# Block-sparse attention with a feed-forward layer on one core: V gathers moved between queues, first save on another queue, second batch's loads dealt out differently

## The chip, the core and the metric

The kernel runs on one core of a Trainium2 chip. A core has a matrix engine (PE), a vector engine (DVE), a scalar engine (ACT), a general engine (POOL, GpSimd), and SP, which here only issues transfers. Each works through its own instructions in order; they meet at semaphores. Transfers (DMAs) are issued by SP, ACT or POOL and carried by 16 DMA engines that all queues share. The metric is the device time in microseconds (us), here the median of three runs.

## The reference

Four batches, eight heads, 768 positions, 64 channels per head. Attention is computed under a block mask (blocks of 32 positions, 24 blocks): a block sees itself and its neighbours, the first and last block see and are seen by everything, and each block also sees three sampled blocks. The heads are put side by side, and a feed-forward layer follows on the 3072 x 512 result.

```python
mask = np.abs(blk_i - blk_j) <= 1
mask = mask | (blk_i == 0) | (blk_j == 0) | (blk_i == n_blocks - 1) | (blk_j == n_blocks - 1)
for qb in range(n_blocks):
    for kb in sampled_blocks[qb]:
        mask[qb*32:(qb+1)*32, kb*32:(kb+1)*32] = True
attn = softmax(np.where(mask, scale * (q @ k.T), -1e9))
x = heads_side_by_side(attn @ v)            # 3072 x 512
h = x @ w_in                                # 3072 x 1024
solu = h * softmax(h)
ln = (solu - mean(solu)) / sqrt(var(solu) + 1e-6) * g_ln
out = ln @ w_out                            # 3072 x 512
```

## The kernel before

**Tiling.** Heads are worked on in pairs, so there are 16 pairs, four to a batch. The program is one list of steps `s`, written out by hand: the loop from L785 goes through them, and whatever a step calls is put on each engine's queue in that order. Six steps make a pair (`SLOT`): in the steps of pair T the static scores are computed (`score_static`, L414: own blocks and first and last block), and in the next six its sampled scores (`score_rand`, L458), the products with V (`out_list` and `out_mms`, L475 and L506) and the division by the sum (`normalise`, L512). From step 33 (`MOE0`) the feed-forward layer's own 120 steps (`moe_step`, L622) are threaded between the attention's, one or two per step.

**Preparing a batch.** V is loaded in six parts of 256 KB (`load_v`), cast to bf16 (`cast_v`), and saved as a whole to a scratch in DRAM, `v_scr` (`save_v`, 780 KB). From there the sampled rows are fetched by block index: 22 query blocks, `inner` (11, three blocks each) and `edge` (11, three sampled and one neighbour), are gathered into the tile `vg` (`gather_v`, L385). A gather is done either on POOL by one indirect DMA with a column of row numbers (L403), or on SP by a load of the indices into registers and three (inner) or four (edge) copies of 32 rows (L396, L400); the argument `on` picks the engine. K and Q are loaded in eight parts of 384 KB (`load_kq`), cast (`cast_kq`), transposed on PE and copied out of the accumulator (`turn_kq`, L317); the sampled K blocks are then copied by index from the transposed K (`gather_k`, L366), most of it on DVE and ACT. `glob_k` and `glob_v` put aside the first and last block.

**What sets the order.** Each queue is in order: an instruction that waits holds all behind it on the same engine. Staging buffers couple the queues. The pool `raw` has four buffers for what is loaded, so the fifth load waits for the cast of the first; `stage` has two for what is cast, so the third cast waits for the first transpose. Each transfer on SP or ACT also takes one of eight semaphores, and waits until the transfer that had it before has landed. The two buffers of `vg` hold batch 0's raw V and raw K and Q first. The feed-forward weights `w_out` are loaded into `w_f`, which lies in the second buffers of the sampled K tiles, so batch 1's `gather_k` waits until they have been scaled (`scale_w`, L655).

**Batch 0** is loaded before the loop: V on SP (L693), then five parts of K and Q (L694 to L696), then four writes of a zero row block to the ends of the scratches (L713), three parts of Q on ACT (L768). V is cast on POOL and ACT in turn and saved on SP (L766). Its gathers stand in steps 2 and 3, odd ones on SP, even ones on POOL. **Batch 1** is prepared from step 4 on (L840 to L866, with `f` the step counted from the batch's start, three steps later for batch 1), on POOL's and SP's queues; batches 2 and 3 the same way 24 and 48 steps later. The weights are loaded at step 7 (`w_out`, `g_ln`, on SP) and step 15 (`w_in`, on POOL).

Of the kernel before, what the change touches and what calls it, by code (L numbers as in the profile page):

```python
# [201 lines left out]
def kernel(  # L202
# [11 lines left out]
    nc = tc.nc  # L214

    B, H, S, D = q.shape
# [85 lines left out]
    def load_kq(b, which, a, eng, rw=None):  # L302

        if rw is None:
            rw = raw.tile([TQ, 2, NT, D], FP32, tag="raw", name=f"raw{which}{b}_{a}")
        eng.dma_start(
            out=rw.rearrange("p h i d -> p h (i d)"),
            in_=(k, q)[which][b, 2 * a : 2 * a + 2].rearrange("h (p i) d -> p h (i d)", i=NT))
        staged[which, b, a] = rw

    def cast_kq(b, which, a, copy):
        rw = staged[which, b, a]
        st = stage.tile([TQ, NT, 2, D], BF16, tag="st", name=f"st{which}{b}_{a}")
        copy(out=st.rearrange("p i h d -> p h i d"), in_=rw)  # L314
        staged[which, b, a] = st
# [17 lines left out]
    def cast_v(b, c, copy):  # L333
        copy(out=vbuf[b % 2][:, c, :, 0:D],  # L334
             in_=staged.pop((2, b, c)).rearrange("p (h d) -> p h d", h=H))

    def save_v(b, lo, hi, eng):
        eng.dma_start(out=v_scr[b][lo * TQ : hi * TQ, :].rearrange("(c p) e -> p c e", p=TQ),
                      in_=vbuf[b % 2][:, lo:hi].rearrange("p c h e -> p c (h e)"))
# [315 lines left out]
    def scale_w(c):  # L655
        nc.vector.tensor_scalar(out=w_out_sb[:, c, :], in0=w_f[c // (KF // 2)][:, c % (KF // 2), :],
                                scalar1=g_ln_sb[:, c : c + 1], scalar2=None, op0=ALU.mult)
# [13 lines left out]
    def centre_w(c):  # L671
        nc.vector.tensor_sub(out=w_out_sb[:, c, :], in0=w_out_sb[:, c, :], in1=mean_sb[0])
# [18 lines left out]
    raw_kq = vgp.tile([TQ, 2 * NPR - 1, 2, NT, D], FP32, tag="vg", name="raw_kq")  # L691
    for c in range(NCH):
        load_v(0, c, nc.sync, raw_v[:, c, :])  # L693
    load_kq(0, 0, 0, nc.sync)  # L694
    for n, (which, a) in enumerate(((1, 0), (0, 1), (0, 2), (0, 3))):
        load_kq(0, which, a, nc.sync, raw_kq[:, n])  # L696
    for vb in vbuf:
        nc.vector.memset(vb[:, :, :, D:D1], 1.0)
    zero_v = prd_p.tile([TQ, 2 * n_ed * BLK], BF16, tag="prd1", name="zero_v")
    nc.vector.memset(zero_v, 0.0)  # L700


    band = setup.tile([TQ, NCH, TQ], BF16, name="band")
# [5 lines left out]
    for z in kgz:  # L709
        nc.vector.memset(z, 0.0)  # L710
    nc.vector.memset(soluT[:, :, :, 128:D2], 1.0)
    for b in range(B):
        nc.sync.dma_start(out=v_scr[b][NB * BLK :, :], in_=zero_v[0:BLK, 0 : H * D1])  # L713


    tab_k = setup.tile([TQ, NB, 4], I32, name="tab_k")
# [46 lines left out]
                                scalar1=sgn * BLK, scalar2=None, op0=ALU.add)  # L763
    for c in range(NCH):
        cast_v(0, c, (nc.gpsimd.tensor_copy, nc.scalar.copy)[c % 2])
    save_v(0, 0, NCH, nc.sync)  # L766
    for a in range(1, NPR):
        load_kq(0, 1, a, nc.scalar, raw_kq[:, 3 + a])  # L768
    for which, a in ((0, 0), (1, 0)):
# [15 lines left out]
    while step < N_STEPS:  # L785
        s += 1
        T, j = s // SLOT, s % SLOT
        pending = len(masks)

        if j < 2 and 1 <= T <= n_pairs:  # L790
            score_rand(T - 1, j)
        if 2 <= j < 5 and T < n_pairs:
            score_static(T, j - 2)

        if 1 <= T <= n_pairs and 1 <= j < 5:
            par = (j - 1) // 2
            if j % 2 == 1:
                lst = out_list(T - 1, par)
                out_mms(lst, 0, 3 * NCH + 1)
            else:  # L800
                out_mms(lst, 3 * NCH + 1, len(lst))
                normalise(T - 1, par)
                if par == 1 and (T - 1) % NPR == NPR - 1:
                    put_rows((T - 1) // NPR)
                    moe_x((T - 1) // NPR * 2)

        mask_all(pending)

        if s >= MOE0:
            for _ in range(2 if (s - MOE0) % 4 == 3 or T > n_pairs else 1):  # L810
                moe_step(step)
                step += 1

        for n in {0: (1, 2), 1: (3, 4), 3: (5,), 4: (6,)}.get(s, ()):
            which, a = ((0, 1), (0, 2), (0, 3), (1, 1), (1, 2), (1, 3))[n - 1]
            cast_kq(0, which, a, nc.vector.tensor_copy)
            turn_kq(0, which, a, (nc.scalar.copy, nc.vector.tensor_copy)[which])
        if s == 1:
            glob_k(0, nc.vector.tensor_copy)
            glob_v(0, nc.vector.tensor_copy)  # L820
        if s in (2, 3):
            for i in range((s - 2) * n_in, n_in + (s - 2) * n_ed):
                gather_v(0, i, on=i % 2)
        if 2 <= s < 6:
            for i in range((s - 2) * 6, min((s - 1) * 6, n_gk)):
                gather_k(0, i, on=(1, 2)[i % 2])

        if s == 15:
            nc.gpsimd.dma_start(out=w_in_sb, in_=moe_w_in.rearrange("(c p) f -> p c f", p=128))
        if s == 7:  # L830
            nc.sync.dma_start(out=g_ln_sb, in_=moe_g_ln.rearrange("(c p) -> p c", p=128))
            load_w()
        if 11 <= s < 11 + KF:
            scale_w(s - 11)
        if s == 24:
            mean_of_w()
        if 25 <= s < 25 + KF:
            centre_w(s - 25)

        for nb in range(1, B):  # L840
            f = s - (nb - 1) * 24
            if f == 4:
                alloc_kq(nb)
            f -= 3 if nb == 1 else 0
            for i in range(6):
                if f == 1 + i // 2:
                    load_v(nb, i, nc.sync)
                if f == 5 + i // 2:
                    cast_v(nb, i, nc.gpsimd.tensor_copy)
            for i in range(8):  # L850
                if f == 4 + i:
                    load_kq(nb, i // 4, i % 4, nc.sync)
                if f == 8 + i:
                    cast_kq(nb, i // 4, i % 4, nc.gpsimd.tensor_copy)
                if f == 11 + i:
                    turn_kq(nb, i // 4, i % 4, (nc.scalar.copy, nc.vector.tensor_copy)[i // 4])
            if f == 9:
                save_v(nb, 0, NCH, nc.sync)
                glob_v(nb, nc.gpsimd.tensor_copy)
            if f == 15:  # L860
                glob_k(nb, nc.gpsimd.tensor_copy)
            for i in range(n_gk):
                if f == 15 + i // 2:
                    gather_k(nb, i, on=(1, 2, 1, 2, 1, 0)[i % 6])
                if f == 12 + i * 13 // 22:
                    gather_v(nb, i, on=(0, 1, 0, 1, 0)[i % 5])  # L866
        if T == n_pairs + 1 and j == 0:
            nc.vector.tensor_scalar(out=okr[:, 0:n_r], in0=recip_all, scalar1=1e-25,
                                    scalar2=None, op0=ALU.is_ge)
            nc.vector.scalar_tensor_tensor(out=okr[:, 0:n_r], in0=recip_all, scalar=1e25,  # L870
                                           in1=okr[:, 0:n_r], op0=ALU.is_le, op1=ALU.mult)
            nc.vector.reduce_sum(out=n_ok[:, 0:1], in_=okr[:, 0:n_r], axis=AX.X)
# [48 lines left out]
```

## Time and profile before

| | |
|---|---|
| median of three runs | 331.94 us (330.65 to 333.08) |
| profiled execution | 334.93 us, of which 333.3 span |
| busy: PE, DVE, ACT, POOL | 231.7, 151.4, 159.1, 98.2 us |
| chain that ended last: PE, DMA, ACT, "issue", DVE | 44, 8, 8, 8 and 6% |
| first feed-forward product on PE (L555) | 121.3 us |
| gathers of V on POOL (L403) | 50, 971 ns each |
| copies of V rows on SP (L396) | 131 |

Times in the profile are us from the span's start, of one profiled execution. A stage is read from what each engine did in it and from what ended its waits; a wait is put down to what ended it last. "issue" is time in which an engine waited for nothing that the profile shows. In the table of stages the columns are length, busy time of PE, PEld (weight load), DVE, ACT and POOL with the number of instructions, granted PE clock, the share of the DMA engines' time and GB/s. In lists by time the columns are start, length, engine, line, instruction, count, and in brackets the idle time before and what ended it; SPq is SP's issuing of transfers.

### The profile page before, as it was taken

To read this page: it belongs to the slowest core of one execution; us is meant where nothing else is said; L and a number is where in the kernel's file an instruction comes from. 1 tells how busy PE (TensorE), PEld (TensorE's weight loads), DVE (VectorE), ACT (ScalarE), POOL (GpSimd) and SP (SyncE) were. 2 spreads that over 40 slices of the span, in tenths; PEclk is the share of its full clock that TensorE was granted. 3 is DMA by queue.
4 is the path that set the end of the run, shared out by engine and by line. 5 is a ranking of instruction groups with operands and counts; after the bars stand their busy time and mean duration, and the time that the engine had idled before them with its cause. 6 is when DMAs were issued, how large, how long until landed. Compare 5 with 4: busy or idle time off the path is not lost.

```text
span 333.3 us, 9097 instructions
## 1 busy us (share of the span) xinstructions
PE 231.7 (70%) x3452; PEld 149.2 (45%) x3466; DVE 151.4 (45%) x488; ACT 159.1 (48%) x328; POOL 98.2 (29%) x151
## 2 busy tenths in 40 slices
PE   0244122808693699946889998567999999889990
PEld 0233121506451456633466566334665755635450
DVE  7667101144460933643475346344644544536250
ACT  2378020408253546622594675236846746233530
POOL 2107500416867442786004337850000000000000
PEclk9999999999556559975899999759999999999998
DMA  7964324999937887455345985442031021043202
GB/s 144 321 227 104 98 53 93 186 384 278 235 86 172 177 244 254 116 107 160 110 99 112 308 273 111 131 130 71 5 80 65 10 74 65 2 112 75 100 30 71
DMA packets 65008, 45.62 MB, mean 137 GB/s; under 512 B 43040, under 2 KB 58752, under 8 KB 64960
## 3 DMA queue, kind: packets, MB, share of 16 engines
q1 hardware_dynamic: 57760, 30.72, 35.6%
q0 software_dynamic: 2928, 6.81, 8.3%
q10 hardware_dynamic: 4272, 7.47, 6.2%
q8 instruction: 28, 0.46, 0.6%
q14 instruction: 20, 0.16, 0.2%
HBM read 33.26 MB, written 9.62 MB: 129 GB/s over the span
## 4 chain that ended last, share of the span: by engine, by line
PE 44%; DMA 8%; ACT 8%; issue 8%; DVE 6%; SPq 4%; another core or an unknown queue 2%; POOL 2%; ACTq 1%; DVEq 0%; POOLq 0%
PE ops L608 11%; PE op L509 10%; PE hps L555 8%; PE sums L573 3%; ACT eT L562 3%; PE ps L468 3%; DMA raw<-in_k_dram 3%; DMA rawv<-in_v_dram 3%; PE tp L321 3%; SPq L396 2%; DMA v_scr<-v 2%; PE ps L437 2%; DVE soluT L563 2%; ACT ot L616 2%
## 5 line engine op out<-in xcount | busy, mean ns | idle before, releaser
L441 ACT ACTIVATE pst<-ps 128x1024 bf16<-128x1024 f32 x48 | 49.1, 1024 | 45.6 <-PE ps L437 36.2
L563 DVE TENSOR_TENSOR soluT<-hps,eT 128x384 bf16<-128x384 f32 x56 | 31.0, 558 | 60.2 <-ACT eT L562 58.7
L403 POOL DMA_INDIRECT vg<-v_scr,idx x50 | 48.5, 971 | 29.4 <-DVE kgi L379 13.8
L321 PE MATMUL tp<-ident,st 128*128 128x128 bf16 x192 | 20.4, 261 | 44.8 <-DVE st L314 14.8
L608 PE MATMUL ops<-w_out_sb,soluT 128*128 128x512 bf16 x179 | 47.2, 408 | 2.4 <-issue 2.0
L555 PE MATMUL hps<-xT,w_in_sb 128*128 128x384 bf16 x224 | 46.4, 334 | 3.4 <-ACT ot L616 2.3
L472 ACT ACTIVATE prd<-ps 96x768 bf16<-96x768 f32 (+1 forms) x32 | 24.0, 755 | 48.7 <-PE ps L468 20.3
L509 PEld LDWEIGHTS <-pst 64*128 64x128 bf16 (+3 forms) x608 | 31.3, 110 | 20.0 <-issue 7.2
L562 ACT ACTIVATE eT<-hps 128x384 bf16<-128x384 f32 x56 | 27.1, 490 | 23.3 <-PE hps L555 22.4
L321 PEld LDWEIGHTS <-st 128*128 128x128 bf16 x192 | 15.1, 116 | 50.0 <-issue 18.0
L520 DVE RECIPROCAL recip_all<-op 128x7 f32<-128x7 f32 x32 | 6.5, 203 | 61.5 <-PE op L509 52.9
L314 POOL CAST st<-raw 128x768 bf16<-128x768 f32 x24 | 20.2, 840 | 33.6 <-DMA raw<-in_k_dram 18.1
L509 PE MATMUL op<-vg,prd 96*32 96x65 bf16 (+1 forms) x704 | 18.8, 211 | 15.1 <-DMA vg<-v_scr 12.1
L509 PE MATMUL op<-v,pst 128*64 128x65 bf16 (+1 forms) x384 | 25.6, 211 | 5.0 <-issue 4.9
L555 PEld LDWEIGHTS <-w_in_sb 128*128 128x128 bf16 x256 | 21.3, 98 | 15.1 <-issue 4.4
L608 PEld LDWEIGHTS <-soluT 128*128 128x128 bf16 x192 | 18.1, 102 | 20.6 <-issue 4.8
L334 POOL CAST v<-rawv 128x512 bf16<-128x512 f32 x18 | 11.4, 654 | 49.5 <-DMA rawv<-in_v_dram 28.1
L324 DVE COPY qT<-tp 128x768 bf16<-128x768 bf16 x15 | 14.3, 953 | 19.4 <-PE tp L321 7.5
L509 PE MATMUL op<-vgl,pst 64*128 64x65 bf16 (+1 forms) x224 | 17.8, 209 | 7.2 <-DVE xb L521 6.2
L509 PEld LDWEIGHTS <-prd 96*32 96x32 bf16 (+1 forms) x704 | 12.6, 104 | 19.9 <-issue 9.9
L324 ACT COPY kT<-tp 128x768 bf16<-128x768 bf16 x16 | 12.7, 803 | 16.7 <-PE tp L321 16.7
L521 DVE TENSOR_TENSOR xb<-op,recip_all 128x448 bf16<-128x448 f32 x32 | 20.0, 624 | 1.2
(106 smaller groups left out, 313.3 us busy)
## 6 DMA issues: line engine op xcount, KB each, us to landing
out_dram<-ot ACTq DMA_DIRECT2D x24, 256.0 KB
raw<-in_k_dram SPq DMA_DIRECT2D x13, 384.0 KB
rawv<-in_v_dram SPq DMA_DIRECT2D x18, 256.0 KB
raw<-in_q_dram SPq DMA_DIRECT2D x12, 384.0 KB
vg<-v_scr SPq DMA_DIRECT2D x131, 32.5 KB
v_scr<-v SPq DMA_DIRECT2D x4, 780.0 KB
w_f<-in_moe_w_out_dram SPq DMA_DIRECT2D x2, 1024.0 KB
raw_v<-in_v_dram SPq DMA_DIRECT2D x6, 256.0 KB
```

The lines of the kernel that those rows point to most:

```text
L314: copy(out=st.rearrange("p i h d -> p h i d"), in_=rw)
L321: nc.tensor.matmul(tp[:, i, :], st[:, i, :], ident, is_transpose=True, start=(i == 0), stop=(i == NT - 1))
L324: copy(out=dst, in_=tp.rearrange("c i p -> c p i"))
L403: nc.gpsimd.indirect_dma_start(out=vgs[b][0:m, i, :], out_offset=None, in_=v_scr[b], in_offset=bass.IndirectOffsetOnAxis(ap=idx[0:m, qb : ...
L441: nc.scalar.activation(out=psts[pair][:, u], in_=ps, func=ACT.Exp, scale=scale)
L472: nc.scalar.activation(out=prds[pair, u], in_=ps[0:m, :, 0 : len(qbs) * BLK], func=ACT.Exp, scale=scale)
L509: nc.tensor.matmul(o, w, m, start=(i == 0), stop=(i == len(lst) - 1), skip_group_check=True)
L521: nc.vector.tensor_tensor(out=xbs[b][:, :, h * D : (h + 1) * D], in0=op[:, :, 0:D], in1=recip.broadcast_to([TQ, NSL, D]), op=ALU.mult)
L555: nc.tensor.matmul(hps, w_in_sb[:, c, f * 128 : (f + 1) * 128], xTs[g][:, c, :], start=(c == 0), stop=(c == KD - 1))
L562: nc.scalar.activation(out=eTs[g, f], in_=hps, func=ACT.Exp, scale=1.0)
L563: nc.vector.tensor_tensor(out=soluT[:, f, :, 0:128], in0=hps.rearrange("p (i x) -> p i x", i=GT), in1=eTs[g, f].rearrange("p (i x) -> p i ...
L608: nc.tensor.matmul(o_ps[t], soluT[:, f, i, 0:128], w_out_sb[:, f, :], start=(f == 0), stop=(f == KF - 1))
```

## The change

- Batch 0's save of V is issued on ACT's queue, behind ACT's casts. The four writes of zero rows come ahead of the K and Q loads on SP.
- Batch 0's gathers of V stand in steps 2 to 5 with its gathers of K, two of three on POOL: 15 on POOL and 7 on SP (11 and 11 before).
- Batch 1: V is loaded in steps 2 to 4, two parts a step, so between SP's gathers, and cast on DVE. K and Q are loaded in steps 5 to 9; K is cast on POOL, Q on DVE, and both are copied out of the accumulator on ACT. The save is at step 7.
- Batch 1's gathers of V run over steps 10 to 26, those of K over steps 21 to 29.
- In batches 1 to 3, too, 15 gathers of V are on POOL and 7 on SP (13 and 9 before).
- In batches 2 and 3 the loads, casts, transposes and gathers of K and Q come a step later, the gathers of V a step earlier.
- `w_out` and `g_ln` are loaded at step 10, behind batch 1's loads, `w_in` at step 12; scaling starts at step 17, the mean is at step 26, and centring takes four steps instead of eight.

```diff
     for c in range(NCH):
         load_v(0, c, nc.sync, raw_v[:, c, :])
-    load_kq(0, 0, 0, nc.sync)
-    for n, (which, a) in enumerate(((1, 0), (0, 1), (0, 2), (0, 3))):
-        load_kq(0, which, a, nc.sync, raw_kq[:, n])
...
     nc.vector.memset(zero_v, 0.0)
+    for b in range(B):
+        nc.sync.dma_start(out=v_scr[b][NB * BLK :, :], in_=zero_v[0:BLK, 0 : H * D1])
+    load_kq(0, 0, 0, nc.sync)
+    for n, (which, a) in enumerate(((1, 0), (0, 1), (0, 2), (0, 3))):
+        load_kq(0, which, a, nc.sync, raw_kq[:, n])
...
-    for b in range(B):
-        nc.sync.dma_start(out=v_scr[b][NB * BLK :, :], in_=zero_v[0:BLK, 0 : H * D1])
...
-    save_v(0, 0, NCH, nc.sync)
+    save_v(0, 0, NCH, nc.scalar)
...
-        if s in (2, 3):
-            for i in range((s - 2) * n_in, n_in + (s - 2) * n_ed):
-                gather_v(0, i, on=i % 2)
         if 2 <= s < 6:
             for i in range((s - 2) * 6, min((s - 1) * 6, n_gk)):
                 gather_k(0, i, on=(1, 2)[i % 2])
-
-        if s == 15:
-            nc.gpsimd.dma_start(out=w_in_sb, in_=moe_w_in.rearrange("(c p) f -> p c f", p=128))
-        if s == 7:
+                gather_v(0, i, on=(0, 1, 0)[i % 3])
+
+        if s == 10:
             nc.sync.dma_start(out=g_ln_sb, in_=moe_g_ln.rearrange("(c p) -> p c", p=128))
             load_w()
-        if 11 <= s < 11 + KF:
-            scale_w(s - 11)
-        if s == 24:
+        if s == 12:
+            nc.gpsimd.dma_start(out=w_in_sb, in_=moe_w_in.rearrange("(c p) f -> p c f", p=128))
+        if 17 <= s < 17 + KF:
+            scale_w(s - 17)
+        if s == 26:
             mean_of_w()
-        if 25 <= s < 25 + KF:
-            centre_w(s - 25)
+        if 27 <= s < 27 + KF // 2:
+            centre_w(2 * (s - 27))
+            centre_w(2 * (s - 27) + 1)
 
         for nb in range(1, B):
             f = s - (nb - 1) * 24
             if f == 4:
                 alloc_kq(nb)
-            f -= 3 if nb == 1 else 0
-            for i in range(6):
-                if f == 1 + i // 2:
+            first = nb == 1
+
+            lv, cv, lk, ck, tk = (2, 4, 5, 8, 9) if first else (1, 5, 4, 8, 11)
+            per = 2 if first else 1
+            pool_copy, dve_copy = nc.gpsimd.tensor_copy, nc.vector.tensor_copy
+            for i in range(NCH):
+                if f == lv + i // 2:
                     load_v(nb, i, nc.sync)
-                if f == 5 + i // 2:
-                    cast_v(nb, i, nc.gpsimd.tensor_copy)
-            for i in range(8):
-                if f == 4 + i:
-                    load_kq(nb, i // 4, i % 4, nc.sync)
-                if f == 8 + i:
-                    cast_kq(nb, i // 4, i % 4, nc.gpsimd.tensor_copy)
-                if f == 11 + i:
-                    turn_kq(nb, i // 4, i % 4, (nc.scalar.copy, nc.vector.tensor_copy)[i // 4])
-            if f == 9:
+                if f == cv + i // 2:
+                    cast_v(nb, i, dve_copy if first else pool_copy)
+            for i in range(2 * NPR):
+                if f == lk + (i + 1) // per:
+                    load_kq(nb, i // NPR, i % NPR, nc.sync)
+                if f == ck + (i + 1) // per:
+                    cast_kq(nb, i // NPR, i % NPR, dve_copy if first and i >= NPR else pool_copy)
+                if f == tk + (i + 1) // per:
+                    turn_kq(nb, i // NPR, i % NPR,
+                            nc.scalar.copy if first or i < NPR else dve_copy)
+            if f == 9 - 2 * first:
                 save_v(nb, 0, NCH, nc.sync)
-                glob_v(nb, nc.gpsimd.tensor_copy)
-            if f == 15:
-                glob_k(nb, nc.gpsimd.tensor_copy)
+                glob_v(nb, pool_copy)
+            if f == 16:
+                glob_k(nb, pool_copy)
             for i in range(n_gk):
-                if f == 15 + i // 2:
+                if f == (21 + i * 9 // n_gk if first else 16 + i // 2):
                     gather_k(nb, i, on=(1, 2, 1, 2, 1, 0)[i % 6])
-                if f == 12 + i * 13 // 22:
-                    gather_v(nb, i, on=(0, 1, 0, 1, 0)[i % 5])
+                if f == (10 + i * 17 // n_gk if first else 11 + i * 13 // n_gk):
+                    gather_v(nb, i, on=(0, 1, 0)[i % 3])
```

## The prediction

> **What bounds the kernel now.** I read the share of busy time by stage first, then PE's waits in the first 94 us, then SP's and POOL's instructions in order of time. Busy time by stage (length, then PE, PEld, DVE, ACT, POOL with counts, granted clock, DMA share, GB/s):
>
> ```profile
> 41.00:57.00 16.00, 3.95 (x54) 2.68 (x52) 0.00 (x0) 2.42 (x3) 0.00 (x0) 1.00 0.24 56
> 65.00:74.00 9.00, 0.00 (x0) 0.00 (x0) 3.41 (x8) 0.61 (x1) 1.48 (x3) 1.00 1.00 351
> 94.00:109.00 15.00, 8.10 (x100) 4.33 (x99) 4.12 (x19) 5.64 (x16) 11.38 (x20) 0.61 0.61 145
> 143.00:157.00 14.00, 8.07 (x96) 4.63 (x96) 5.03 (x17) 3.77 (x11) 11.31 (x20) 0.62 0.53 140
> 157.00:207.00 50.00, 45.74 (x770) 30.14 (x770) 25.68 (x78) 33.71 (x67) 15.22 (x21) 0.97 0.62 168
> ```
>
> From the first product of the second half (121.3 us) on, PE is nearly full (45.7 of 50) except where POOL's gathers run back to back. Before that, two stages leave it empty. PE's waits (total, times, longest), first for 20 to 57 us, then for 57 to 94:
>
> ```profile
> PE op L509 <- DMA vg<-v_scr: 12.1, 6, 2.2
> ...
> PE tp L321 <- POOL st L314: 13.6, 3, 9.3
> ```
>
> The first is the wait for batch 0's V gathers, the second for batch 1's K and Q. Both hang on SP's queue (start, length, instruction, count):
>
> ```profile
> 19.65 0.39 SPq L338 DMA_DIRECT2D v_scr<-v  x1
> 23.69 22.17 SPq L396 DMA_DIRECT2D vg<-v_scr  x21
> ...
> 55.12 0.41 SPq L400 DMA_DIRECT2D vg<-v_scr  x1
> 55.58 5.33 SPq L329 DMA_DIRECT2D rawv<-in_v_dram  x6
> 60.97 2.36 SPq L831 DMA_DIRECT2D g_ln_sb<-in_moe_g_ln_dram  x1
> 63.38 1.64 SPq L649 DMA_DIRECT2D w_f<-in_moe_w_out_dram  x2
> 65.12 2.51 SPq L306 DMA_DIRECT2D raw<-in_k_dram  x4
> ```
>
> So the chain is: v saved at 19.65, gathers from 23.69 to 55.5, then v loads, weights, and only at 65.12 the first K of batch 1. And 22 us for 21 copies is not SP's own pace. The same row asked in three windows (24 to 29, 29.2 to 40.7, 41 to 55):
>
> ```profile
> 23.69 5.06 SPq L396 DMA_DIRECT2D vg<-v_scr  x9
> ...
> 30.86 5.73 SPq L396 DMA_DIRECT2D vg<-v_scr  x3
> ...
> 40.88 4.97 SPq L396 DMA_DIRECT2D vg<-v_scr  x8
> ```
>
> 0.56 us per copy (5.06 over 9) before and after, but between 28.75 and 40.88 only four copies, 3.0 us each. The instruction records there show SP's register moves at 0.70 us against 0.04 elsewhere, later the same on DVE, and PE matmuls 0.5 us apart with nothing waited for. It coincides with POOL's streak of gathers:
>
> ```profile
> 24.89 1.46 POOL L403 DMA_INDIRECT vg<-v_scr,idx  x1 [13.77 <-DVE kgi L379]
> ...
> 37.96 0.95 POOL L403 DMA_INDIRECT vg<-v_scr,idx  x1 [0.30 <-issue]
> ```
>
> The crawl begins some 4.3 us after the streak's first gather and ends 2.0 us after its last (38.91). 94 to 109 and 143 to 157 are the same: nine gathers in a row, PE half empty. The trace doesn't say why; I use it as a measured price. It can't be the profiler alone: the executions without a profile are only 3.0 us shorter.
>
> **Part 1: first save on ACT, tail rows ahead of the loads.** Batch 0's casts end at 12.22 (ACT). SP issues the save at 19.65 only because the four tail-row writes before it waited. On ACT it issues near 12.3, costing ACT one issue (0.39) ahead of three loads. Alone it took 4.0 us (19.65 to 23.69). Now it shares the engines with eight 384 KB loads: it lands between 16.3 and, if all 3.1 MB went first at the page's 321 GB/s, 25.9. I take 20.0, since two queues drain together. The gathers then start 3.7 us earlier. The loads may end 2.4 us later (0.78 MB at 321 GB/s); batch 0's K gathers on ACT and DVE (from 22.2 and 22.8) move with them, covered by the wait for V. SP's four writes now stand before the K load, 4 x 0.4 = 1.6 us, while raw_v still drains until 11.6: 0 on the path, at most 1.6.
>
> [...]
>
> **Part 2: batch 0's gathers, POOL 15 (was 11), SP 7 (was 11).** POOL: 0.95 + 0.30 idle = 1.25 each, 1.46 the first. It started 1.2 us after SP, so 21.2 + 1.76 + 14 x 1.25 = 40.5, landing by 42.5. SP: 12 copies for four inner blocks, 12 for three edge blocks, six v loads between. The crawl now lasts from 21.2 + 4.3 = 25.5 to 42.5. Until 25.5 SP does 8 copies and two loads; in the 17 us of crawl at 3.0 each some 4 copies and two loads; then three edge gathers at 2.30 (45.91 to 48.21) and two loads, 7.8 us: issued by 50.3, landed by 52.3. The last use by PE was at 57.1, so **4.8 us won**. The K gathers of ACT and DVE fall into the crawl more than before; at most half of their eleven are left at 42.5, 6 x 0.8 = 5 us, ready at 48: still before V. Bounds: without a crawl POOL is last, 42.5, 14.6 won; if v4 and v5's loads, which wait for DVE casts behind slowed K gathers, hold SP, 0 won.
>
> **Part 3: batch 1's loads between the gathers, weights behind.** First K load at 50.3 instead of 65.12. It took 8.3 us to its cast (73.42) behind 2 MB of weights; in batch 2, with none, 3.4 us (118.12 to 121.49). Cast 53.7, while PE reaches its transpose some 3 us after 52.3, at 55. So the **9.3 us wait goes**; late next is Q, whose loads wait for POOL's casts (buffers) and SP's v save, near 57, cast on DVE by 61. PE, with pair 0's 7.6 us and eight transposes at 0.82, needs the last near 66. Bounds: 9.3, or 6 if Q is late.
>
> PE's second wait (3.6 us before 85.76) was a Q cast on POOL behind a gather that waited 3.55 for v's save. Now K is cast before the gathers and Q on DVE: **3.6 won**. DVE takes ten casts more, 4 x 0.56 and 6 x about 0.4 = 4.6 us, and was busy 15.6 of 37 us between 57 and 94: hidden. ACT takes four copies more (0.80 each, on DVE 0.95): hidden likewise, ACT was busy under two thirds. Weights issue near 59; scaling waits for 1 MB, about 68, and PE comes there near 72: 0, at most 4 if w_in on POOL's queue delays it. Their cover is those three steps of PE work.
>
> **Part 4: the later streaks.** PE idles 6.9, 5.9 and 7.5 us in the three of before (94 to 109, 143 to 157, 207 to 230), 6.8 on average for nine gathers in a row, 0.76 each. Batch 1 now has 15 with hardly a cast between: 15 x 0.76 = 11.3, **4.5 lost**. Batches 2 and 3 keep nine after the zeroed K tile; the two more stand among casts. 0, at most 2 x 1.5 each. Their casts, transposes and K gathers come one step later, the last four steps before use: 0.
>
> [...]
>
> PE's clock I count at 0: six transposes take 0.82 us at 74 us and 0.49 at 126, so a stage with fewer holes may run faster, and the longer streak slower; PE is busy 15.2 us from 74 to 94, and 5 of them are the most that a warmer clock could give.
>
> **Sum.** -4.8 - 9.3 - 3.6 + 4.5 = -13.2. The profiled execution took 334.93 (span 333.3), so 321.7; the median lies 3.0 lower, 331.94, so **318.7**.
>
> **Rivals.**
> - *Slower: the streak costs more than it did.* If in batches 1 to 3 all 15 gathers cost PE 1.0 us each, 45 us against 20.3 now, 24.7 lost, 17.7 won: 339. It decides from 0.84 a gather. For it: PE nearly stopped from 33.7 to 40.9; against: gathers with a cast between (84 to 90) show no crawl. 17%.
> - *Half:* SP crawls on, the first pair ends at 57 as now, Q is late: 0 + 6 + 3.6 - 4.5, 327. 16%.
> - *Nothing left:* the same, and the weights hold DVE 4 us: 331. 8%.
> - *More:* the crawl comes from SP's copies meeting POOL's streak, and with fewer copies there is none in batch 0 and no more than now in batch 1: 14.6 + 9.3 + 3.6 won, 304.4. 12%.
> - Forecast: 47%, 312 to 324.
>
> A change of less than 1% can't be told from none here. So faster by over 1%: 47 + 16 + 12 = 0.75; within 1%: 0.08; slower: 0.17. The range, 305 to 336, leaves out about half of "more" and a little over half of "slower", 0.16 in all.
>
> **What would show it.** Save on ACT's queue near 12.3; first gather near 20; PE's last vg wait near 52; SP's first K load near 50; no wait of PE for st above 3 us; first hps near 108 (121.3 now); PE idle about 11 us in batch 1's streak, near 60 to 82; the rest unchanged. Wrong if the crawl isn't tied to POOL's streak, or if K gathers, not V, hold the first pair.

## The result, and the profile after

The change makes next to no difference: **330.84 us** (median of 13 runs, 326.13 to 334.75) against 332.7 (13 runs, 330.26 to 334.94), a ratio of medians of 0.994. Forecast were 318.7 us, 4.0% less. The ratios with intervals below count only runs within 1.5% of a kernel's fastest, here 7 of the changed kernel's 13 and all 13 of the kernel before; by that count the ratio is 0.9868, with a 95% interval of 0.9824 to 0.9911. Measured twice more in later lots the unchanged pair gave 0.9999 (0.9955 to 1.0043) and 0.9965 (0.9921 to 1.0009). So the gain lies between nothing and 1.3%, under the 2% from which a difference is called one here. A *lot* is here a set of kernels run one after the other on one chip, beside the kernel before; ratios are always within a lot.

The profiled execution took 333.61 us, span 332.0, against 334.93 and 333.3. Two later profiles of the changed kernel (e10 and e17 below) have its first division and its first hps (both explained below) within 0.4 us. First the stages (columns as in the prediction):

```profile
42.50:57.00 14.50, 6.29 (x111) 4.67 (x111) 8.93 (x41) 7.51 (x24) 1.48 (x4) 1.00 0.47 105
57.00:74.00 17.00, 12.26 (x164) 9.12 (x164) 4.52 (x9) 8.95 (x11) 8.32 (x10) 1.00 1.03 327
84.30:98.20 13.90, 6.68 (x92) 4.51 (x88) 3.02 (x12) 4.26 (x12) 10.57 (x16) 1.00 0.64 154
143.00:157.00 14.00, 9.45 (x109) 4.79 (x107) 2.84 (x11) 4.82 (x13) 11.46 (x21) 0.88 0.69 171
157.00:207.00 50.00, 44.43 (x741) 29.07 (x741) 28.66 (x89) 32.08 (x65) 17.01 (x25) 0.97 0.58 159
```

The empty stage of before at 65 to 74 is filled, and the one around POOL's *streak* (gathers one behind the other) is now at 84 to 98, as empty as it was. ACT's issue of the save, then SP's instructions:

```profile
11.98 0.43 ACTq L338 DMA_DIRECT2D v_scr<-v  x1
...
7.76 2.52 SPq L699 DMA_DIRECT2D v_scr<-zero_v  x4
...
21.80 3.28 SPq L396 DMA_DIRECT2D vg<-v_scr  x6
25.12 1.04 SPq L329 DMA_DIRECT2D rawv<-in_v_dram  x2
26.71 14.36 SPq L396 DMA_DIRECT2D vg<-v_scr  x6
41.09 2.79 SPq L329 DMA_DIRECT2D rawv<-in_v_dram  x2
...
51.19 1.02 SPq L329 DMA_DIRECT2D rawv<-in_v_dram  x2
52.75 1.50 SPq L396 DMA_DIRECT2D vg<-v_scr  x3
54.30 0.41 SPq L400 DMA_DIRECT2D vg<-v_scr  x1
54.80 1.93 SPq L306 DMA_DIRECT2D raw<-in_k_dram  x4
```

The crawl is there again, 14.36 us for six copies (0.55 us each ahead of it). It ends at 44, behind POOL's last gather at 41.4. The first K load comes at 54.80 instead of 65.12. PE's waits from 20 to 57; then two instructions of PE and, between them in time, VectorE's (DVE's) around the one that matters:

```profile
PE tp L321 <- DVE st L314: 18.3, 2, 16.9
PE tp L321 <- issue: 4.0, 1, 4.0
...
PE op L509 <- DMA vg<-v_scr: 1.0, 1, 1.0
```

```profile
28.71 0.82 PE L321 MATMUL tp<-ident,st 128*128 128x128 bf16 x6 [4.03 <-issue]
56.20 0.29 PE L509 MATMUL op<-vg,prd 128*32 128x65 bf16 x3 [0.97 <-DMA vg<-v_scr]
```

```profile
28.10 0.56 DVE L314 CAST st<-raw_kq 128x768 bf16<-128x768 f32 x1
43.99 0.96 DVE L324 COPY qT<-tp 128x768 bf16<-128x768 bf16 x1 [15.34 <-remote]
...
52.33 0.18 DVE L383 COPY kge<-kT 128x128 bf16<-128x128 bf16 x1
56.54 0.20 DVE L520 RECIPROCAL recip_all<-op 128x7 f32<-128x7 f32 x1 [0.65 <-PE op L509]
```

This is the heart of it. The wait for V, 12.1 us before, is 1.0. In its place DVE stands still for 15.34 us inside the crawl, ahead of a copy of Q, and its gathers of K end at 52.5 instead of the 48 of the prediction. The six transposes that this copy reads had ended at 29.5, so DVE did not wait for work of PE; the profile names no releaser ("remote"). PE's 16.9 us ahead of its next transposes are the same hole, passed on by the cast that stands behind the copy on DVE. V is late as well: SP's loads at 51.19 had waited 3.0 us for DVE's casts of v, which stand among the K gathers, the four copies of its last gather (52.75 and 54.30) went out behind them, and PE's last wait for V ended at 56.20 (57.1 before, 52.3 forecast). So K and V both hold the first pair, and the first division (the reciprocal, L520) comes at 56.5 against 57.2. I use divisions as milestones from here on: one ends each half pair.

### The profile page after: what moved, and what is told of

It is laid out like the page before. It is cut to its first block, busy times and chain, and to the rows that moved or that the text cites. A ratio compares the mean times of both kernels' runs of the same rounds, so it can differ in the third digit from the quotient of the medians.

```text
span 332.0 us, 9018 instructions
## 1 busy us (share of the span) xinstructions
PE 235.3 (71%) x3466; PEld 150.1 (45%) x3466; DVE 154.0 (46%) x494; ACT 161.9 (49%) x332; POOL 100.8 (30%) x151
## 4 chain that ended last, share of the span: by engine, by line
PE 44%; DVE 13%; DMA 10%; ACT 9%; issue 9%; another core or an unknown queue 8%; SPq 2%; ACTq 1%; DVEq 1%; POOL 0%; POOLq 0%
PE op L509 12%; PE ops L608 9%; PE hps L555 8%; PE ps L468 4%; ACT eT L562 3%; DMA raw_kq<-in_q_dram 3%; PE sums L573 3%; DMA raw<-in_q_dram 2%; DVE xb L521 2%; PE ps L437 2%; PE tp L321 2%; ACT ot L616 2%; ACT pst L441 2%; DVE soluT L563 2%
## 5 line engine op out<-in xcount | busy, mean ns | idle before, releaser
L441 ACT ACTIVATE pst<-ps 128x1024 bf16<-128x1024 f32 x48 | 49.0, 1024 | 44.3 <-remote 20.7
L403 POOL DMA_INDIRECT vg<-v_scr,idx x60 | 57.2, 953 | 33.9 <-issue 14.3
L608 PE MATMUL ops<-w_out_sb,soluT 128*128 128x512 bf16 x192 | 48.9, 400 | 2.5 <-DVE qT L324 1.6
L555 PE MATMUL hps<-xT,w_in_sb 128*128 128x384 bf16 x224 | 48.2, 344 | 2.8 <-ACT ot L616 1.7
L520 DVE RECIPROCAL recip_all<-op 128x7 f32<-128x7 f32 x32 | 6.5, 202 | 49.5 <-PE op L509 28.9
L555 PEld LDWEIGHTS <-w_in_sb 128*128 128x128 bf16 x256 | 21.5, 100 | 15.1 <-issue 5.0
L314 POOL CAST st<-raw 128x768 bf16<-128x768 f32 x20 | 16.8, 840 | 29.4 <-DMA raw<-in_k_dram 13.4
L324 DVE COPY qT<-tp 128x768 bf16<-128x768 bf16 x11 | 10.5, 955 | 32.0 <-remote 26.4
L509 PE MATMUL op<-v,pst 128*64 128x65 bf16 (+1 forms) x384 | 24.8, 213 | 0.5 <-issue 0.5
L509 PE MATMUL op<-vg,prd 96*32 96x65 bf16 (+1 forms) x704 | 17.7, 211 | 6.0 <-issue 5.1
L452 DVE TENSOR_TENSOR pst<-pst,band 128x1024 bf16<-128x1024 bf16 (+1 forms) x32 | 20.2, 631 | 0.7 <-ACT pst L441 0.6
L437 PE MATMUL ps<-qT,kT 64*128 64x128 bf16 (+1 forms) x384 | 19.4, 230 | 0.4 <-PE op L509 0.4
L545 PEld LDWEIGHTS <-eT 128*128 128x128 bf16 x192 | 11.9, 98 | 15.9 <-ACT eT L562 10.7
```

Source lines behind the costliest of these rows:

```text
L403: nc.gpsimd.indirect_dma_start(out=vgs[b][0:m, i, :], out_offset=None, in_=v_scr[b], in_offset=bass.IndirectOffsetOnAxis(ap=idx[0:m, qb : ...
L437: nc.tensor.matmul(ps[:, par, col : col + w], kT[:, c * TQ : (c + 1) * TQ], rhs, start=first, stop=(n == len(todo) - 1), skip_group_check= ...
L441: nc.scalar.activation(out=psts[pair][:, u], in_=ps, func=ACT.Exp, scale=scale)
L452: nc.vector.tensor_tensor(out=psts[pair][:, u, :, 0:w], in0=psts[pair][:, u, :, 0:w], in1=band[:, 4 * u : 4 * u + n, :].rearrange("p c (o ...
L509: nc.tensor.matmul(o, w, m, start=(i == 0), stop=(i == len(lst) - 1), skip_group_check=True)
L555: nc.tensor.matmul(hps, w_in_sb[:, c, f * 128 : (f + 1) * 128], xTs[g][:, c, :], start=(c == 0), stop=(c == KD - 1))
```

## Experiments

All of them add nothing to what is computed and leave nothing out. "Stall" is the word below for the crawl on the engines beside POOL, whose own gathers keep their pace in it (0.92 to 1.12 us each and 0.30 apart in the changed kernel's profile).

### Is POOL's streak the cause, and what in it?

Three theories: R, gathers following each other at 1.25 us; G, any indirect gather on POOL; M, SP's copies meeting POOL's gathers (the rival "More"). One lot, the kernel before at 337.72 us there, one execution each. The four edits in batch 0, from the changed kernel's line:

```diff
-                gather_v(0, i, on=(0, 1, 0)[i % 3])
+                gather_v(0, i, on=(0, 1, 0)[i % 3])     # e1: as it was, and behind each gather of POOL
+                if i % 3 != 1:
+                    for _ in range(3):
+                        nc.gpsimd.tensor_copy(out=fill, in_=fill)   # spare tile, 128 x 256
+                gather_v(0, i, on=0)                    # e2: all on POOL
+                gather_v(0, i, on=i % 2)                # e3: 11 and 11
+                gather_v(0, i, on=1)                    # e4: all on SP
```

> The changed kernel with three small POOL copies (some 1 us together, on a spare tile) behind each of batch 0's 15 POOL gathers, so that these follow each other at about 2.1 us instead of 1.25. Theory R (rate: the crawl comes of indirect gathers that follow each other at 1.25 us): no crawl in batch 0, the long PE wait near 30 to 47 us is gone, K gathers end near 38, the first division on DVE comes when POOL's last gather has landed, near 57 (56.5 now). Theory G (any indirect gathering on POOL slows the others, from some 4 us after its first gather to 2 us after its last): the crawl lasts to about 56, first division near 66. Theory M (SP's copies meeting POOL's gathers): crawl as long as SP has copies left, to about 45.

> The changed kernel with all 22 of batch 0's V gathers on POOL, none on SP. R and G: the streak lasts 22 x 1.25 = 27.5 us, the crawl to about 52, K gathers after it, first division near 62 to 65. M: no crawl in batch 0, K gathers end near 38, first division near 54, when the last gather has landed.

> The changed kernel with batch 0's V gathers split as before, odd ones on SP, even ones on POOL (11 and 11). R and G: the streak ends 5 us earlier, the crawl near 39 instead of 43; K gathers end near 48, but SP has 39 copies instead of 24 and ends near 57; first division near 58. M: the crawl lasts at least as long as now, to 43 or more.

> The changed kernel with all 22 of batch 0's V gathers on SP, none on POOL. All three theories: no crawl in batch 0, K gathers end near 38; SP issues 77 copies at 0.57 and six loads, 47 us, so its last gather lands near 70, first division near 71, batch 1's first K load near 69; the whole some 10 us longer than the changed kernel. If there is a crawl here all the same, POOL isn't its cause.

Measured: 337.7, 337.02, 335.9 and 347.7 us. The times say little, the profiles much. POOL and SP with the spaced gathers (e1):

```profile
22.54 1.41 POOL L403 DMA_INDIRECT vg<-v_scr,idx  x1 [11.46 <-DMA raw_kq<-in_q_dram]
23.96 1.34 POOL L830 COPY fill<-fill 128x256 bf16<-128x256 bf16 x3
25.46 0.97 POOL L403 DMA_INDIRECT vg<-v_scr,idx  x1 [0.16 <-issue]
```

```profile
26.46 3.45 SPq L396 DMA_DIRECT2D vg<-v_scr  x6
...
42.41 2.16 SPq L306 DMA_DIRECT2D raw<-in_k_dram  x4
```

The same 15 gathers at 2.5 us apart: six SP copies take 3.45 us again, not 14.36; K's gathers on DVE end at 40.6 instead of 52.5, and SP's first K load is at 42.41 instead of 54.80. G falls. POOL's own last gather, at 60, now holds the first division (62.0), so the total doesn't move. With all 22 on POOL (e2) SP makes no copies and the stall is longer, the wait ahead of DVE's copy of Q 19.33 us; M falls:

```profile
53.82 0.96 DVE L324 COPY qT<-tp 128x768 bf16<-128x768 bf16 x1 [19.33 <-remote]
```

With 11 (e3) POOL's streak is 22.7 to 36.5 and the first division 58.8; with none on POOL (e4) there is no stall in batch 0, DVE's K gathers end at 39.8, but SP alone takes until 71 and the first division is at 73.2. Of the three, R stands. One thing is not separated: a copy between two gathers stops the stall, but whether the time that it takes does it or the copy as such, no run here tells.

### Spacing by batch, and the schedule without parts 1 and 2: a lot that doesn't stall

```diff
     nc.gpsimd.indirect_dma_start(
         out=vgs[b][0:m, i, :], out_offset=None, in_=v_scr[b],
         in_offset=bass.IndirectOffsetOnAxis(ap=idx[0:m, qb : qb + 1], axis=0))
+    if b == 1:                      # e5; e6 and e7: every batch
+        for _ in range(2):          # e7: 1
+            nc.gpsimd.tensor_copy(out=fill, in_=fill)
...
-                gather_v(0, i, on=(0, 1, 0)[i % 3])
+                gather_v(0, i, on=i % 2)                     # e6
+                gather_v(0, i, on=(0, 1, 0, 1, 0)[i % 5])    # e7: 13 and 9
```

e8 is the changed kernel with the save, the zero rows, the loads and the gathers of batch 0 as before: parts 3 and 4 alone.

> The changed kernel with two small copies of a spare tile (128 x 256, about 0.45 us each) behind every GpSimd gather of the second batch alone; batch 0 stays as it is. Rate theory (gathers that follow each other at 1.25 us slow every other engine's instructions, spaced ones do not): the stretch from 88 to 101, in which TensorE is busy 4.8 of 13 us, goes back to a normal one (TensorE about 10 of 13), the divisions 84.2 to 98.2 come within 6 us of each other instead of 14, the first matmul of hps moves from 119.7 to 111-114, and the whole is 5 to 8 us shorter than the changed kernel (0.965 to 0.975 of before). Rival P (the lost stretch was GpSimd's casts and the late second copy of kgz, not the streak): the divisions keep their 14 us, hps stays at 119-121, the time within 1% of the changed kernel. Rival Q (won and then paid back): hps near 112, but the end less than 2 us earlier, with a new wait for V of the second batch.

> The changed kernel with two spare-tile copies behind every GpSimd gather of every batch, and the gathers of batch 0 dealt 11 to GpSimd and 11 to SP. Rate theory: pitch about 2.1 us, no crawl in any batch; K gathers of batch 0 done at 40, GpSimd's and SP's V gathers at 45-48, first division 49-52 (56.5 in the changed kernel), second-batch loads from about 48, first hps 104-109, the later batches' streaks gone too: 305 to 318 us where before takes 333-338 (0.92 to 0.95). Rival (the late batches have slack for their streaks): hps 104-109 but the end only 8 to 12 us under before (0.965 to 0.975). Rival (GpSimd becomes the bound by the 110 us-odd of added copies in 60 gathers' shadow, about 54 us): V of the third or fourth batch is waited for, and the time is within 1% of before.

> As the run with two copies, but with one copy behind each GpSimd gather (pitch about 1.7 us) and batch 0 dealt 13 to GpSimd and 9 to SP. It tells where the crawl begins. If 1.7 us is slow enough: no register move at 0.7 us, K gathers done at 40, V at 44-47, first division 48-51, within 1% of the run with two copies. If it is too fast: register moves near 0.7 us from about 4 us after the first gather on, K gathers done after 48, first division 54-57, and 1 to 3% above the run with two copies.

> The changed kernel with the save back on SP's queue, the zero rows and batch 0's K and Q loads in their old order, and batch 0's V gathers as before (11 and 11, in two steps ahead of the K gathers): the second batch's schedule and the weights alone. My theory (what the early loads win is lost again in the second batch's streak): first division 57-58 as before, first K load of the second batch about 57-60 (65.1 before), no wait over 4 us for the transposes, then the streak takes 13 us for two half pairs; first hps 118-122, time 0.985 to 1.0 of before. Rival (the early loads are worth their 13 us, and batch 0's gathers lose it): hps near 110, 0.96 to 0.97 of before. Rival (nothing without the freed SP queue): first K load still at 65, 1.0 to 1.02.

Measured: 302.84, 311.88, 302.84 and 303.23 us, and **305.98 for the kernel before**, 26 us less than the median that the prediction started from. Ratios 0.9886 (0.983 to 0.9942), 1.0223 (1.0156 to 1.029), 0.9897 (0.9837 to 0.9958), 0.9931 (0.9893 to 0.9969). In none of the four profiles is there a register move of 0.7 us, and in e5, whose batch 0 is the changed kernel's untouched, 15 gathers run from 22.6 to 41.3 as in the changed kernel, and the first division comes at 44.7 instead of 56.5. So the same instructions at the same rate do not stall here. Nor are ACT and DVE faster by themselves in this lot: ACT's exponentials of L441 take 1024 ns on average in the changed kernel's profile and 1025 in e5's (where it is L444), DVE's casts of v 424 ns on average in the former and 0.43 us each in e8's.

These runs then answer a different question than asked: what spacing costs where it buys nothing. Two copies behind each gather make POOL late for its own K gathers of batch 1 (PE waited 13.5 us for them in e5). And e8 shows a coupling that the prediction did not have: with batch 0's gathers left as they were, part 3's casts of v on DVE stand between DVE's K gathers and wait for SP's loads, which stand behind SP's V copies.

```profile
50.97 0.43 DVE L334 CAST v<-rawv 128x512 bf16<-128x512 f32 x1 [8.88 <-DMA rawv<-in_v_dram]
...
54.82 0.20 DVE L520 RECIPROCAL recip_all<-op 128x7 f32<-128x7 f32 x1
```

The first division had to wait for DVE itself. Parts 3 and 4 are worth 0.7% without parts 1 and 2, where nothing stalls.

### The pair again, part 1 alone, and a version that is better

e9 and e10 are the two kernels unchanged, e11 is the kernel before with part 1 alone (the diff's lines on zero rows, K loads and the save). e12 is e7 with the second batch's three K gathers taken from POOL:

```diff
-                    gather_k(nb, i, on=(1, 2, 1, 2, 1, 0)[i % 6])
+                    gather_k(nb, i, on=(1, 2)[i % 2] if first else (1, 2, 1, 2, 1, 0)[i % 6])
```

> The kernel before, unchanged, for its profile beside the other kernels of this lot. Two chips gave 332-338 us for it and another 306. Stall theory (the difference is the stretches in which GpSimd's back-to-back gathers slow every engine's instructions): where it takes near 306, no register move of 0.7 us anywhere, first division 54-56, first hps 107-111, and TensorE's waits put down to nothing (issue) under 3 us after that; where it takes near 335, register moves of 0.7 us about 4 us after the first gather, first division 57, hps 121. Rival (that chip is faster in everything): the single instructions are shorter too, in proportion, 8 per cent.

> The changed kernel, unchanged. On a chip that takes near 306 us for the kernel before: no stall; first division 44-46, first K load of the second batch 41-43, hps 102-106, and 0.98 to 0.99 of before: the 10 us that batch 0 wins are given back before hps, where the second batch's K gathers on GpSimd queue behind its V gathers. If the prediction's sum was right but for the stall, it is 0.955 to 0.97. On a chip near 335: as measured, 0.98 to 0.99, first division 56-57.

> The kernel before with the first part alone: zero rows ahead of the K loads, and the first v written back on ScalarE's queue. My step: gathers start 3 to 4 us earlier (20-22.5 for 24.9), nothing on ScalarE is late for it, SP's V copies and its second-batch K load move as much, and the end moves 1.5 to 4 us: 0.988 to 0.995. Rival (the K loads behind the zero rows delay the Q transposes and K gathers as much): first division within 1 us, 0.997 to 1.003.

> The changed kernel with one spare-tile copy behind every GpSimd gather (pitch 1.7 us), batch 0 dealt 13 to GpSimd and 9 to SP, and the second batch's three K gathers taken from GpSimd (to ScalarE and VectorE). On a chip near 306 us: TensorE no longer waits for K of the second batch behind GpSimd (7 us with the pacing, in the run before), hps 96-99, 0.97 to 0.98. Near 335 us: if 1.7 us is slow enough for no stall, first division 47-51, hps 98-104, 305 to 312 us (0.91 to 0.93); if stalls come at 1.7 us as well, first division 55-58 and 0.96 to 0.99.

This lot stalls: the kernel before took 335.26 us over 19 runs (e9's own four: 338.95). The changed kernel 334.52, ratio 0.9999 (0.9955 to 1.0043). Part 1 alone 332.65, **0.9873** (0.9825 to 0.992; medians 0.992): more than the whole change in this lot. Its profile has 0.8 us of that before the first feed-forward product (119.7 against 120.5 in e9); where the rest comes from I can't show, as e9's profiled execution was among the longest of its kernel (339.33 us).

e12 took **309.7 us, 0.9254** (0.9183 to 0.9324). Its rows on POOL and SP:

```profile
24.63 0.94 POOL L403 DMA_INDIRECT vg<-v_scr,idx  x1 [0.17 <-issue]
25.58 0.40 POOL L408 COPY fill<-fill 128x256 bf16<-128x256 bf16 x1
26.15 0.98 POOL L403 DMA_INDIRECT vg<-v_scr,idx  x1 [0.17 <-issue]
```

```profile
29.82 3.16 SPq L396 DMA_DIRECT2D vg<-v_scr  x6
```

One small copy of 0.40 us behind each gather, gathers 1.5 us apart in these rows (1.6 on average over batch 0), and six copies on SP take 3.16 us. First division 47.5, first hps (the first feed-forward product, L555 in the kernel before) 105.1 (119.9 in e10). In this lot the threshold lies between 1.25 and about 1.5 to 1.6 us; e12 is not wholly free of it, with one register move of 0.7 us in batch 0 and 4.7 us of PE's waits between 60 and hps put down to nothing (9.7 in e10).

### Each batch's term, and the kernel before with the same copies

e13 and e18 are the kernel before with one copy behind every POOL gather (two lots). In the changed kernel: e14 spaces batch 0 alone (13 and 9), e15 batch 1 alone (with its K gathers off POOL), e16 batches 2 and 3 alone. e17 is the changed kernel.

> The kernel before with one spare-tile copy behind every GpSimd gather, nothing else. Theory S (the stalls are in both kernels and cost both about 20 to 30 us, so what the change itself is worth is hidden under them): where the unpaced kernel takes near 335, this takes 311 to 318 (0.93 to 0.95), and the changed kernel with the same copies (309.7 in the lot before) is 1 to 2.5 per cent under it. Rival T (the change opened the way, and spacing pays on it alone): 325 to 335 (0.97 to 1.0). Where the unpaced kernel takes near 306: 0.99 to 1.01.

> The changed kernel, batch 0's V gathers dealt 13 to GpSimd and 9 to SP with one copy behind each of GpSimd's, the other batches as they are. Theory (terms add): first division 47-48 (56.8), the 9 us stay up to hps (110-112 for 119.9) and to the end: 322 to 327 us where the changed kernel takes 331 to 334.5, 0.965 to 0.98 of before. Rival (the second batch's streak takes them back): hps 117-120 and within 1 per cent of the changed kernel. Near 306: 0.985 to 0.995.

> The changed kernel, one copy behind each GpSimd gather of the second batch alone, and that batch's three K gathers moved from GpSimd to ScalarE and VectorE. Theory (terms add): first division 56-57 as in the changed kernel, the 14 us between two divisions in the streak fall to 6-9, hps 113-115, the end 5 to 6 us earlier: 0.975 to 0.985 of before. Rival (the stretch is K gathers queueing, not the stall): hps 118-121 and no gain. Near 306: 0.98 to 0.99.

> The changed kernel, one copy behind each GpSimd gather of the third and fourth batch alone. Theory (terms add): hps 119-121 as in the changed kernel, then 30-31 us instead of 37.5 to the division that ends the second batch, 33 instead of 39.5 in the fourth's: 318 to 323 us (0.955 to 0.97 of before). Rival U (the late streaks stand in slack): within 1 per cent of the changed kernel. Near 306: 0.985 to 1.0.

> The changed kernel, unchanged. Where the kernel before takes near 306, the runs with only some batches spaced say: no stall, first division 44-46, first K load of the second batch 41-42, hps 97-100, 293 to 298 us, 0.955 to 0.97 of before: the 4 per cent of the prediction. If instead the gain needs the spacing: 0.98 to 1.0, 301 to 306 us. Where the kernel before takes near 335: 0.985 to 1.0 again, first division 56-57, hps 119-120.

> The kernel before with one spare-tile copy behind every GpSimd gather. Where the unpaced kernel takes near 335: by the theory that both kernels lose 20 to 30 us to their streaks, 312 to 319 us (0.93 to 0.955), no register move of 0.7 us, first division 50-52, hps 112-115; by the rival (spacing pays on the changed kernel alone) 325 to 335. Where it takes near 306: 1.01 to 1.02 again, 310 to 313 us.

The lot of e13 to e16 does not stall (before: 306.82 us), that of e17 and e18 does (335.84).

| | lot | time, us | ratio to before |
|---|---|---|---|
| e13 before, spaced | no stall | 312.29 | 1.0156 (1.0087 to 1.0225) |
| e14 changed, batch 0 spaced | no stall | 294.71 | 0.9596 (0.9531 to 0.9661) |
| e15 changed, batch 1 spaced | no stall | 294.15 | 0.9564 (0.9497 to 0.9631) |
| e16 changed, batches 2, 3 spaced | no stall | 297.38 | 0.9668 (0.9593 to 0.9742) |
| e17 changed | stall | 333.81 | 0.9965 (0.9921 to 1.0009) |
| e18 before, spaced | stall | 313.91 | 0.9408 (0.9324 to 0.9491) |
| e12 changed, spaced | stall | 309.7 | 0.9254 (0.9183 to 0.9324) |

e18 settles theory S against T: the kernel before loses 22 us to its own streaks. Spaced, the two kernels stand 1.6% apart (0.9254 over 0.9408; two lots, and e12 has its other edits too). e14 to e16 were to tell the terms of the stall apart and could not, since nothing stalled. For such a lot I had put down 1 to 2% at most, taking the early runs e5 and e7 for the rule, and missed: each has large unspaced parts of the changed kernel in it, and each is 3.3 to 4.4% faster than before. The changed kernel itself never ran in such a lot. An estimate from several traces: e16 is the changed kernel up to 106 us (first hps at 97.4). Batches 2 and 3 are the changed kernel's in e5, e8, e14 and e15, which took 193.4 to 197.1 us from their first hps to the end (e14 193.5). e14's time was 1.6 us longer than its span. Together 292 to 296 us, 0.953 to 0.965 of 306.82.

The milestones side by side (us from the span's start; "lot" says whether the unspaced kernel stalls there; the fifth and sixth divisions enclose most of batch 1's streak in the changed kernel):

| kernel, lot | first division | fifth and sixth | first hps | first division to hps | hps to end |
|---|---|---|---|---|---|
| before, stall | 57.2 | 87.8, 93.5 | 121.3 | 64.1 | 212.0 |
| changed, stall | 56.5 | 84.2, 98.2 | 119.7 | 63.1 | 212.3 |
| e13, no stall | 49.9 | 82.1, 88.0 | 112.8 | 62.9 | 202.6 |
| e18, stall | 48.2 | 78.9, 86.2 | 110.8 | 62.6 | 201.1 |
| e12, stall | 47.5 | 72.7, 79.9 | 105.1 | 57.6 | 201.1 |
| e16, no stall | 45.1 | 70.5, 74.7 | 97.4 | 52.3 | 199.5 |
| e14, no stall | 46.5 | 72.6, 76.7 | 99.5 | 53.0 | 193.5 |

The waits of PE in that half pair of the changed kernel, 84 to 98.5, and the stage row of the same half pair in e16:

```profile
PE ps L468 <- issue: 6.7, 11, 1.2
```

```profile
70.60:74.70 4.10, 3.65 (x67) 2.37 (x63) 2.96 (x12) 2.67 (x6) 1.56 (x3) 0.50 0.25 57
```

The one needs 13.9 us, 6.7 of them with PE waiting for nothing that the profile shows, the other 4.2, and that at half the granted clock.

## Why the prediction was wrong, step by step

**Part 1: right in place, late by 1.6 us.** The save left ACT at 11.98 and had landed by 21.6 (20.0 forecast, bounds 16.3 to 25.9); the first gather on POOL was at 22.76, 2.1 us earlier than before instead of 3.7.

**Part 2: 0.6 us won instead of 4.8; this step failed.** The step is "at most half of their eleven are left at 42.5, 6 x 0.8 = 5 us, ready at 48: still before V". It took what was left as bare work. Each group of gathers on DVE stands behind a copy of Q, and DVE was held ahead of that copy for 15.34 us, 14.5 of them with the transposes done: K ready at 52.5. And as DVE's casts of v stand among these gathers, SP's loads of v4 and v5 waited for them and V, forecast for 52.3, was there at 56.2. The text named both: K gathers that hold the first pair as what would make it wrong, the loads behind slowed K gathers as the bound "0 won". e1 confirms it from the other side: spaced, K is ready at 40.6.

**Part 3: the waits went, but not all of them.** Between 57 and 94, PE's waits for batch 1's casts were 13.6 us in one row before. After, they are 4.2:

```profile
PE tp L321 <- DVE st L314: 3.6, 3, 2.4
...
PE tp L321 <- POOL st L314: 0.6, 1, 0.6
```

So 9.4 won where 12.9 were put down. The part that stayed is Q, late as the rival "half" had it: its loads went out at 59.14 to 63.7. That is not for the late first K load alone: in e16, where nothing stalls and K's loads start at 41.34, 3.7 us ahead of the first division (1.7 here), PE waits 3.4 and 0.6 us at the same places. SP's Q loads wait there for POOL's casts of K, 2.7 us, and here 2.9; the prediction named that wait, with 3.3 us as its bound, and counted it at nothing.

**Part 4: 8.4 us lost instead of 4.5.** From the first division to the first hps the whole gained 1.0 us (64.1 to 63.1; in the pair e9 and e10 0.3); with 9.4 won, 8.4 went again, by subtraction. The price of the new streak, 11.3, was near, but by luck: it was counted for 15 gathers in a row near 60 to 82. POOL did five from 68.5 on, waited, and did ten from 86.0 to 99.7, the first six with nothing between:

```profile
85.16 0.61 POOL L355 COPY kgz<-kT 64x256 bf16<-64x256 bf16 x1 [9.47 <-DMA vg<-v_scr,idx]
```

Against e16 the stage is 10.8 us longer (63.1 against 52.3), 9.7 of them in the one half pair of these ten. What failed is the 6.8 subtracted as the old streak's price. That was PE's idle time in its window, and idle time is not price: some of it would have been spent on other waits. Nor were the nine gathers of before a row: K copies of 0.8 us stand behind the first, the fourth and the seventh (at 95.51, 99.90 and 104.38). The spaced kernels before, 62.6 and 62.9, are only 1.2 to 1.5 us shorter in this stage than the unspaced, though they pay for the copies there as well (e13's PE waits 2.8 us for a K gather on POOL), so the true price lies above that; 10.8 less the 8.4 leaves 2.4, an estimate that takes the rest of the stage as unchanged.

**Batches 2 and 3: 0 forecast, 0.3 lost** (212.0 and 212.3). Right, but not because they are free: without stall this stretch takes the changed kernel 193.4 to 197.1 us (e5, e8, e14, e15), so that it loses 15 to 19 us in it. The kernel before loses at least 9 (202.6 in e13, copies included).

**The sum.** -0.6 - 9.4 + 8.4 + 0.3 = -1.3, the difference of the spans. The forecast of -13.2 misses by 4.2 in part 2, 3.5 in part 3, 3.9 in part 4 and 0.3 in the rest.

**Rivals.** The time fell on "nothing left" (331), in part by luck: its first two steps are seen (first pair at 56.5, Q late), but not its third: no wait of PE for the weights stands in the profile. "More" had the wrong cause (e2). "Slower" was right that a streak without casts costs more, in batch 1 alone (9.7 us for ten gathers, where it put 1.0 each).

**The point of method.** I took the crawl as a fixed stretch laid over the schedule and priced each engine's work under it by itself. But it holds several engines at once (between 26 and 46 us of the changed kernel's profile six SP copies take 14.36 us, DVE stands still for 15.34 and ACT for 14.2, in two waits), and one that is held holds what stands behind it on the others: DVE's one hole made K late, and through the casts of v also SP's copies of V. Where it is absent, the kernel before has its first division at 49.9 (e13, spaced) and the changed one at 45.1 (e16). That these are 4.8 apart, as forecast, shows little, as e13 has the copies' cost in it; but the estimate of 0.953 to 0.965 stands around the forecast 0.960. So without the stall the schedule seems to be worth about what the bookkeeping said, though the pair was not run there. Under the stall, the gain is spent on more back-to-back gathers.

## What to carry to other kernels

When a profile shows unrelated engines slow at the same time, find what is common before moving work under it; here, in a lot that stalls, one 0.4 us copy behind each GpSimd gather was worth 22 us on the kernel before (335.84 to 313.91, e18), five times the best that the change gave. Idle time of an engine inside a disturbed stretch is not its price: by the estimates above 6.8 us of PE's were worth 2.4 in the kernel before, and 7.2 (13.90 less 6.68 busy, in the half pair from 84 to 98) were worth 9.7 in the changed one. Ask what the engine would have waited for next, and compare with a run in which the stretch is not disturbed. And compare only within one lot, and repeat a small gain in a second one: the same pair gave 0.987, 1.000 and 0.997 by the same count.

## What the hardware showed that I had not expected

**Gathers close behind each other on one engine can slow the others.** In a lot that stalls, fifteen indirect gathers on GpSimd at 1.25 us bring register moves on SP from 0.04 to 0.70 us and leave 202 instructions recorded on the core between 22.5 and 43 us (e10); at 2.5 us there are 556 (e1), with none on GpSimd 542 (e4). It looks like a step rather than slower work: between 28 and 44 us of the changed kernel's trace SP's instructions start 0.7 us or twice that apart, nearly all of them (29.10, 29.81, 31.21, 32.62, 33.35, 34.06).

**It isn't always there.** In two of the five lots the same program at the same rate did not stall (563 instructions in that window in e16), and the kernel before took 306 us instead of 333 to 338. Part of what looks like the kernel's time is thus the lot's. It is not the chip alone: the record has chip 11 for the lot of e5 to e8 (before: 305.98 us) and for that of e9 to e12 (335.26 us). What sets it I could not find out, and no run here tries to force it.

**Why it stalls is open.** The transfers' own times don't tell: the median packet of GpSimd's queue between 26 and 44 us took 159 ns where it stalls (e10) and 161 where it does not (e16). The prediction argued that it can't be the profiler alone, as unprofiled executions are only 3.0 us shorter; that argument is weaker than it read, since every time listed comes with a span and a granted clock, so something, it seems, was recorded in each. By what mechanism the gathers slow the other engines, no run here shows.

**Spacing costs where nothing stalls**: 1.6% on the kernel before (e13), and in batches 2 and 3 of the changed kernel some 2 to 6 us (199.5 in e16 against 193.4 to 197.1 unspaced). A kernel for both kinds of lot may do well to space where GpSimd has time to spare; e15, spaced in batch 1 alone, took 294.15 us, within the estimate for the changed kernel, and was not run where it stalls.
